# Item loads of an RWKV attention stage: one long row per partition split into two shorter pieces

## The chip, the core and the metric

The kernel runs on one core of a Trainium2 chip. The core has a matrix engine (TensorE, PE in the profile; its weight loads are listed as PEld), a vector engine (VectorE, DVE), a scalar engine (ScalarE, ACT), GpSimd (POOL) and SyncE (SP), which here does nothing but issue DMAs. Sixteen DMA engines move data between HBM (the chip's main memory) and SBUF (the on-chip memory, 128 partitions), and they also bring the engines' own instructions. PSUM holds what PE writes. The metric is the device time of one execution in microseconds, as the median of several runs.

## What is computed

Two blocks follow each other. The first is a linear attention with a decaying state (RWKV-5), for B = 4 sequences, H = 8 heads, S = 768 tokens and D = 48 channels per head:

```python
for t in range(S):
    kt, vt, rt = (k[:, :, t], v[:, :, t], r[:, :, t])
    cur = np.einsum('bhd,bhe->bhde', u[None] * kt, vt)
    y[:, :, t] = np.einsum('bhd,bhde->bhe', rt, state + cur)
    state = w[None, :, :, None] * state + np.einsum('bhd,bhe->bhde', kt, vt)
```

Its output, with heads side by side, is x with 384 channels per token. The second block is a mixture of experts with a gate that keeps neighbours together:

```python
fresh_e = int(np.argmax(logits[b, s]))
if s == 0 or local_gate[b, s] < 0.5:
    e = fresh_e
else:
    e = prev_e if prev_e >= 0 else fresh_e
...
h = np.maximum(x[b, s] @ w1[e], 0.0)
out[b, s] = p[e] * (h @ w2[e])
```

There are 8 experts with 1024 hidden channels; p is the softmax of the token's 8 logits.

## The kernel before

**Two stages.** The first stage computes the attention, item by item, and routes the tokens of the first two sequences on the way. The second stage gathers tokens by expert and runs the experts' two matrix products; it is PE's alone, nearly without a gap. The order of the instructions on every engine is written out by hand (`tc.manual_schedule()`), so nothing is moved by a scheduler; an engine starts its next instruction when the semaphores that it waits for are there.

**Items.** An item is one sequence and one pair of heads: 4 x 4 = 16 items. The two heads of a pair lie in partitions 0 to 47 and 64 to 111 (padded to 64 each). The 768 tokens are cut into six chunks of 128. For each item the kernel needs three inputs, which the host lays out before the run:

- `rk`: r and k with channels in the partitions, 768 tokens of r and then 768 of k in a row: 6144 bytes per partition, 768 KB in all
- `kv`: k and v with tokens in the partitions, 576 numbers each and 16 of padding: 4672 bytes per partition, 584 KB
- `vT`: v with channels in the partitions, 3072 bytes per partition, 384 KB

**Loads.** `load(n)` (lines 194 to 206) issues the three DMAs of item n on SP's queue: rk (line 199, or for item 0 two halves, line 202), kv (line 203), vT (line 204). Items 0 to 2 are loaded at the start, and item n + 3 at the top of step n. There are four buffers each for rk and vT and five for kv. A load into a used buffer waits for the old item's last reader. Apart from that, SP's DMAs share eight completion semaphores in turn, so a load also waits for the landing of the DMA that was issued eight before it. Each load is cut by partitions over the 16 DMA engines, eight partitions each; in the packet records every partition's row is one packet, and each engine ends a DMA with a packet of 4 bytes for the semaphore.

**An item's work.** In the order of the data:

- POOL, `scale` (lines 208 to 229): `ke`, k times a decay (line 217, from kv, two halves); `rw`, r times a decay (line 234, from rk, two halves; for items 0 to 2 on DVE); `pd`, r times k (line 221, from rk, two halves). For items from 3 on the order is ke, rw, pd, one item ahead of PE.
- DVE, `keys`: `kw`, k times the inverse decay (line 241, from rk).
- PE, `added` (line 253, from ke and kv): each chunk's addition to the state; DVE, `states` (line 259): the scan over the chunks.
- PE, `scores` (line 289, from kw and rw): scores inside a chunk, in two halves of three chunks; DVE masks each half (line 291).
- PE, `own` (line 269, from pd) and DVE (line 274, with vT): the token's own term. It stands between the two halves of the scores from item 3 on.
- PE, `inside` (line 298, from the masked scores and kv) and `before` (line 311, from the state and rw); ACT and DVE copy the result out (line 315), PE transposes it (line 324), ACT copies it to x (line 326) and, once per sequence, stores x to HBM (line 329, on ACT's own DMA queue).

The instructions of one item run interleaved with those of its neighbours: step n has `added`, `keys` and `states` of item n, `scale` of item n + 1, `inside` and `before` of item n - 1, then `scores` and `own` of item n.

**Code.** PE alone has over 7,700 matmuls and weight loads. They are not repeated by a loop, so PE's program comes from HBM while it runs, as packets of 16 KB on a queue of their own (q8 in the profile).

**The rare path.** `general_attention` (from line 473) is run only when a decay lies outside the bounds of the fast path. It reads the same arrays and is not entered with this data.

Of the kernel before, what the change touches and what calls it, by code (L numbers as in the profile page):

```python
# [50 lines left out]
C2 = NCH // 2  # L51
AHEAD = 4
VB = NCH * 2 * DH


def spread(ap, axis, n):
# [5 lines left out]
class Attention:  # L62
# [13 lines left out]
    def __init__(self, tc, st, rk_d, kv_d, vT_d, x_d, w_t, wp_d, kept, ident, lt, mp):  # L76
        self.tc, self.nc = tc, tc.nc
        nc = tc.nc
        self.rk_d, self.kv_d, self.vT_d, self.x_d = rk_d, kv_d, vT_d, x_d
        self.w_t, self.kept, self.ident, self.lt = w_t, kept, ident, lt  # L80

        self.late = st.enter_context(tc.tile_pool(name="late", bufs=1))
        self.wp = self.late.tile([P, H, 32], F32, name="wp")
        self.sel = self.late.tile([P, 2 * (E + 1)], F32, name="sel")
        self.inner = ExitStack()

        def pool(name, bufs, **kw):
            return self.inner.enter_context(tc.tile_pool(name=name, bufs=bufs, **kw))

        once = pool("once", 1)  # L90
        self.two = pool("two", 2)
        self.three = pool("three", 3)
        ps = pool("ps", 1, space=PSUM)

        self.pairs = [ps.tile([P, 2, 512], F32, name=f"pair{i}") for i in range(2)]
        self.py = pool("py", 1, space=PSUM)

        self.T = mp[:, 2 * P + 2:2 * P + 2 + (NCH - 1) * DH].rearrange("p (e c) -> p e c", c=NCH - 1)

        self.inv = pool("pinv", 1, space=PSUM).tile([P, HP, P], F32, name="inv")  # L100


        n = B * HP - 1
        self.rks, self.vTs = [None] * AHEAD, [None] * AHEAD
        for i in range(1, AHEAD + 1):
            self.rks[(n + i) % AHEAD] = once.tile([P, 2, NCH, P], F32, name=f"rk{i}")
        for i in range(1, AHEAD + 1):
            self.vTs[(n + i) % AHEAD] = once.tile([P, 2, C2, P], F32, name=f"vT{i}")
        self.kvs = [once.tile([P, 2 * VB + DP - DH], F32, name=f"kv{i}") for i in range(AHEAD + 1)]
        self.items = [dict() for _ in range(B * HP)]  # L110
        self.xTs, self.xs, self.lTs = {}, {}, {}
        for i in range(AHEAD - 1):
            self.load(i)
        nc.sync.dma_start(out=self.wp, in_=wp_d)


        self.step = once.tile([P, HP, DH, NCH - 1], F32, name="step")
        nc.vector.memset(self.step, 0.0)


        self.tab = tab = once.tile([P, HP, 2, P + 1], F32, name="tab")
        nc.vector.memset(tab[:, 0, :, 0:1], 1.0)
        nc.gpsimd.memset(tab[:, 1:, :, 0:1], 1.0)
        w = once.tile([P, HP, 2], F32, name="w")
        nc.vector.tensor_scalar(w[:, :, 0], w_t[:, :, 0], W_LO, W_HI, Alu.max, Alu.min)
        nc.vector.reciprocal(w[:, :, 1], w[:, :, 0])
        nc.vector.tensor_copy(tab[:, 0, :, 1], w[:, 0])
        nc.gpsimd.tensor_copy(tab[:, 1:, :, 1], w[:, 1:])
        n = 2
        while n <= P:  # L130
            m = min(n - 1, P + 1 - n)
            for engine, t in ((nc.vector, tab[:, :1]), (nc.gpsimd, tab[:, 1:])):
                engine.tensor_mul(t[..., n:n + m], t[..., 1:1 + m], t[..., n - 1:n].to_broadcast([P, t.shape[1], 2, m]))
            n += m

        self.first, self.newton = mp[:, :P + 1], mp[:, P + 1:2 * P + 1]
        nc.scalar.copy(self.first, tab[:, 0, 0])
        self.reciprocals(0)

        self.end = once.tile([P, HP, P + DP], F32, name="end")  # L140
        self.endT = once.tile([P, 2, HP, 2 * DH], F32, name="endT")
        self.align(26)
        self.warm(8)
        self.ends(slice(0, 1))
        self.turn_ends(slice(0, 1))
        self.warm(5)
# [47 lines left out]
    def load(self, n):  # L194
        nc = self.nc
        b, hp = divmod(n, HP)
        rk, vT, kv = self.rks[n % AHEAD], self.vTs[n % AHEAD], self.kvs[n % (AHEAD + 1)]
        if n:
            nc.sync.dma_start(out=rk.rearrange("p a c t -> p (a c t)"), in_=self.rk_d[b, hp])
        else:  # L200
            for z in (slice(0, C2), slice(C2, NCH)):
                nc.sync.dma_start(out=rk[:, :, z], in_=self.rk_d[b, hp].rearrange("p (a c t) -> p a c t", a=2, c=NCH)[:, :, z])
        nc.sync.dma_start(out=kv, in_=self.kv_d[b, hp])
        nc.sync.dma_start(out=vT.rearrange("p a c t -> p (a c t)"), in_=self.vT_d[b, hp])
        self.items[n].update(b=b, hp=hp, rT=rk[:, 0], kT=rk[:, 1], vT=vT,
                             k=kv[:, :VB].rearrange("p (c x) -> p c x", c=NCH), v=kv[:, VB:])

    def scale(self, n):

# [263 lines left out]
def general_attention(tc, rk_d, kv_d, wu, wg_d, x_d, ident, lt):  # L473

    nc = tc.nc
    with tc.tile_pool(name="g1", bufs=1) as g1, tc.tile_pool(name="g2", bufs=2) as g2, \
# [9 lines left out]
        with tc.For_i(0, HP, 1) as hp:  # L486
            wu_t = g1.tile([P, 2], F32, name="g_wu")
            nc.sync.dma_start(out=wu_t, in_=wu[bass.ds(hp, 1)].rearrange("o p x -> (o p) x"))
            with tc.For_i(0, B, 1) as b:
                def of(ap):  # L490
                    return ap[bass.ds(b, 1), bass.ds(hp, 1)].rearrange("o q p x -> (o q p) x")

                r_t = g1.tile([P, S], F32, name="g_r")
                k_t = g1.tile([P, S], F32, name="g_k")
                v_t = g1.tile([P, NCH, 2, DH], F32, name="g_v")
                nc.sync.dma_start(out=r_t, in_=of(rk_d)[:, :S])
                nc.sync.dma_start(out=k_t, in_=of(rk_d)[:, S:])
                nc.sync.dma_start(out=v_t.rearrange("p c i e -> p (c i e)"),
                                  in_=of(kv_d)[:, 2 * NCH * DH:4 * NCH * DH])
                yp = gy.tile([P, 2, 512], F32, name="g_y")  # L500
                for e in range(DH):
                    vp = gps.tile([P, 2, 512], F32, name="g_vp")
                    for c in range(NCH):
                        for i in range(2):
                            nc.tensor.matmul(
                                vp[i * DP:(i + 1) * DP, c // 3, (c % 3) * P:(c % 3 + 1) * P],
                                lhsT=v_t[:, c, i, e:e + 1].to_broadcast([P, DP]),
                                rhs=turned if c % 2 else ident,
                                start=True, stop=True)
                    kv = g2.tile([P, S], F32, name="g_kv")  # L510
                    nc.vector.tensor_mul(kv.rearrange("p (g t) -> p g t", g=2),
                                         k_t.rearrange("p (g t) -> p g t", g=2), vp[:, :, :3 * P])
                    sv = g2.tile([P, S + 1], F32, name="g_sv")
                    nc.vector.memset(sv[:, 0:1], 0.0)
                    nc.vector.tensor_tensor_scan(sv[:, 1:], wu_t[:, 0:1].to_broadcast([P, S]), kv, 0.0,
                                                 Alu.mult, Alu.add)
                    z = g2.tile([P, S], F32, name="g_z")
                    nc.vector.scalar_tensor_tensor(z, kv, wu_t[:, 1:2], sv[:, :S], Alu.mult, Alu.add)
                    nc.vector.tensor_mul(z, z, r_t)
                    for c in range(NCH):  # L520
                        o = (c % 3) * 2 * DH + 2 * e
                        nc.tensor.matmul(yp[:, c // 3, o:o + 2], lhsT=z[:, c * P:(c + 1) * P], rhs=ones,
                                         start=True, stop=True)
                y = g1.tile([P, 2, 3, 2, DH], F32, name="g_ys")
                for g in range(2):
                    for i in range(2):
                        nc.vector.tensor_copy(
                            y[:, g, :, i, :],
                            yp[:, g, :6 * DH].rearrange("p (c e i) -> p c e i", c=3, i=2)[:, :, :, i])
                nc.sync.dma_start(  # L530
                    out=x_d.rearrange("(b c p) (h j) -> b h p c j", b=B, p=P, h=HP)
                    [bass.ds(b, 1), bass.ds(hp, 1)].rearrange("o q p c j -> (o q p) c j"),
                    in_=y.rearrange("p g c i e -> p (g c) (i e)"))
# [1113 lines left out]
def _rows(a, np):  # L1647

    x = np.pad(a.transpose(0, 1, 3, 2), ((0, 0), (0, 0), (0, DP - DH), (0, 0)))
    return x.reshape(B, HP, P, S)  # L1650
# [50 lines left out]
```

## Time and profile before

| what | value |
|---|---|
| median of 3 runs | 389.7 us (389.01 to 390.44) |
| the profiled execution | 389.11 us |
| its span, first instruction to last | 387.0 us |
| busy: PE, PEld | 369.1 us (95%), 329.6 us (85%) |
| busy: DVE, ACT, POOL | 256.5, 102.9, 150.7 us |
| DMA in the whole span | 17477 packets, 74.97 MB |
| SP's queue (q1) | 10048 packets, 56.89 MB |
| ACT's queue (q10), GpSimd's (q0) | 7.87 MB, 9.52 MB |
| instruction queue q8 | 32 packets, 0.52 MB |
| rk, kv, vT: issue to landing, median | 9.8, 8.9, 8.1 us |
| last item load issued, landed | 85.14, 90.11 us |

How to read it: the span is what the trace covers, from the first of the program's instructions to the last; the execution's own time is 2.1 us longer. A line such as L217 is line 217 of the kernel. In a timeline a row has a start, a duration, the engine, the line, the operation and what it writes and reads; in square brackets stands how long the engine was idle before it, and who ended the wait ("issue" is idle time for which the profile finds no releaser). The granted clock is the share of PE's full clock that the chip allowed. A DMA's packets are listed by queue; the trace also keeps for every packet its queue, size, start and duration.

### The profile page before, as it was taken

The numbers are of one execution on the slowest core, as the hardware profiler recorded it, in microseconds if no ns is written. First come the engines' busy times: TensorE is split into PE (matmuls) and PEld (weight loads), VectorE is DVE, ScalarE is ACT, GpSimd is POOL, SyncE is SP. The second block draws the span as 40 slices with busy tenths as digits, with TensorE's granted clock in tenths as the row PEclk, the third lists the DMA queues.
The fourth block names the chain that finished last, engine by engine and source line by source line (L and its number), as shares of the span: only waits on it lengthen the run. The fifth ranks groups of instructions, "written<-read, shape, count | busy, mean of one in ns | idle before, by whom it ended". The sixth has DMA issues, their size and how long they took to land. (4 is left out here: it accounts for less than half of the span.)

```text
span 387.0 us, 9749 instructions
## 1 busy us (share of the span) xinstructions
PE 369.1 (95%) x3858; PEld 329.6 (85%) x3858; DVE 256.5 (66%) x749; ACT 102.9 (27%) x293; POOL 150.7 (39%) x212
## 2 busy tenths in 40 slices
PE   8998999799989999999999999999999999999992
PEld 7776876677868999998999999999999999999971
DVE  6997686899974573587647757757767758556400
ACT  4121221122213111322323243234224234222220
POOL 8769999696322022611233212312403213112022
PEclk9999999999999999999999999999999999999997
DMA  7999998989212982640453145245156146064011
GB/s 266 413 409 411 405 403 272 315 294 400 86 31 94 374 337 75 246 189 23 184 167 120 41 169 205 74 171 203 55 185 224 38 163 225 23 200 182 2 37 36
DMA packets 17477, 74.97 MB, mean 194 GB/s; under 512 B 2729, under 2 KB 6586, under 8 KB 14864
## 3 DMA queue, kind: packets, MB, share of 16 engines
q1 hardware_dynamic: 10048, 56.89, 39.4%
q0 software_dynamic: 3424, 9.52, 7.4%
q10 hardware_dynamic: 3952, 7.87, 5.6%
q8 instruction: 32, 0.52, 0.5%
q14 instruction: 21, 0.17, 0.1%
HBM read 64.83 MB, written 9.51 MB: 192 GB/s over the span
## 5 line engine op out<-in xcount | busy, mean ns | idle before, releaser
L1259 POOL DMA_INDIRECT out_dram<-yo,sid x27 | 26.7, 988 | 102.7 <-ACT yo L1254 79.0
L1110 PE MATMUL h<-exT,w1t 128*128 128x168 f32 (+4 forms) x240 | 54.9, 327 | 0.0
L1114 DVE TENSOR_TENSOR hT<-h,hs 128x168 f32<-128x168 f32 (+3 forms) x60 | 21.1, 351 | 46.4 <-PE h L1110 30.0
L1033 POOL DMA_INDIRECT xg<-x_d,gid x29 | 31.2, 1076 | 39.3 <-DVE sm L868 17.4
L1110 PEld LDWEIGHTS h<-exT,w1t 128*128 128x128 f32 x240 | 41.6, 190 | 0.3 <-issue 0.3
L1060 PE MATMUL h<-exT,w1t 128*128 128x192 f32 (+1 forms) x192 | 38.2, 337 | 0.0
L1179 PE MATMUL y<-factors,sums 128*128 128x192 f32 x168 | 36.8, 326 | 0.0
L1110 PE MATMUL h<-xs,ws 128*128 128x168 f32 (+4 forms) x144 | 35.3, 326 | 0.0
L1060 PEld LDWEIGHTS h<-exT,w1t 128*128 128x128 f32 x192 | 32.3, 190 | 1.4 <-issue 0.2
L221 POOL TENSOR_TENSOR pd<-rk 128x384 f32<-128x384 f32 x32 | 31.4, 1002 | 2.3 <-DMA rk<-in_rk_dram 2.3
L291 DVE TENSOR_TENSOR am<-pair,kept 128x768 f32<-128x768 f32 x32 | 30.3, 949 | 1.4 <-PE pair L289 1.4
L1110 PEld LDWEIGHTS h<-xs,ws 128*128 128x128 f32 x144 | 25.5, 190 | 4.3 <-ACT hs L1117 1.2
L1179 PEld LDWEIGHTS y<-factors,sums 128*128 128x128 f32 x168 | 28.9, 190 | 0.0
L289 PEld LDWEIGHTS pair<-rw,kw 48*64 48x64 f32 x768 | 23.7, 133 | 5.4 <-issue 1.6
L289 PE MATMUL pair<-rw,kw 48*64 48x64 f32 (+1 forms) x768 | 26.4, 249 | 1.2 <-issue 1.0
L234 POOL TENSOR_TENSOR rw<-rk,tab 128x384 f32<-128x384 f32 x26 | 23.6, 926 | 8.2 <-PE y L311 8.2
L217 POOL TENSOR_TENSOR ke<-kv,endT 128x288 f32<-128x288 f32 x32 | 24.9, 797 | 4.3 <-DMA kv<-in_kv_dram 3.0
L298 PE MATMUL y<-am,kv 128*64 128x128 f32 x384 | 25.3, 276 | 0.5 <-DVE am L291 0.4
L1179 PE MATMUL y<-w2t,hT 128*128 128x192 f32 x96 | 23.0, 328 | 0.0
L298 PEld LDWEIGHTS y<-am,kv 128*64 128x64 f32 x384 | 21.0, 137 | 1.9 <-DVE am L291 0.9
L1047 DVE COPY exT<-tp 128x384 f32<-128x384 f32 (+6 forms) x29 | 14.0, 488 | 12.8 <-PE tp L1046 12.6
L1165 DVE TENSOR_TENSOR factors<-w2t 128x192 f32<-128x192 f32 x56 | 19.7, 351 | 0.0
(279 smaller groups left out, 733.5 us busy)
## 6 DMA issues: line engine op xcount, KB each, us to landing
w1t<-in_w_dram SPq DMA_DIRECT2D x9, 1536.0 KB, 6.7
w2t<-in_w_dram SPq DMA_DIRECT2D x9, 1536.0 KB, 6.9
rk<-in_rk_dram SPq DMA_DIRECT2D x15, 768.0 KB, 9.8
kv<-in_kv_dram SPq DMA_DIRECT2D x16, 584.0 KB, 8.9
vT<-in_vT_dram SPq DMA_DIRECT2D x16, 384.0 KB, 8.1
x_d<-x ACTq DMA_DIRECT2D x4, 1152.0 KB, 8.6
w1t<-in_w_dram ACTq DMA_DIRECT2D x1, 1536.0 KB, 10.5
w2t<-in_w_dram ACTq DMA_DIRECT2D x1, 1536.0 KB, 13.6
```

The lines of the kernel that those rows point to most:

```text
L217: nc.gpsimd.tensor_mul(t["ke"][:, p::2], t["k"][:, p::2], spread(self.endT[:, p, hp], 1, C2))
L221: nc.gpsimd.tensor_mul(t["pd"][:, z], t["rT"][:, z], t["kT"][:, z])
L234: engine.tensor_mul(t["rw"][:, z], t["rT"][:, z], spread(pw, 1, z.stop - z.start))
L289: nc.tensor.matmul(sc[f * DP:(f + 1) * DP, h, i, x:], lhsT=t["kw"][q, c, o * DP:(o + 1) * DP], rhs=t["rw"][q, c, x:], start=True, stop=True)
L291: return lambda: nc.vector.tensor_mul(t["am"][:, g], sc, spread(self.kept[:, g:g + 3], 1, 2))
L298: nc.tensor.matmul(t["y"][h][p * DP:(p + 1) * DP, c2 * P:(c2 + 1) * P], lhsT=t["v"][:, (2 * c + h) * DH:(2 * c + h) * DH + DP], rhs=t["am" ...
L1033: self.nc.gpsimd.indirect_dma_start(out=xg[:n], out_offset=None, in_=self.x_d[:rows], in_offset=bass.IndirectOffsetOnAxis(ap=u["gid"][:n, ...
L1060: nc.tensor.matmul(h[:, :n], lhsT=u["w1"][:, m, kk, :], rhs=u["xT"][:, kk, :], start=(kk == 0), stop=(kk == DK - 1))
L1110: nc.tensor.matmul(out, lhsT=a, rhs=b, start=start and k == 0, stop=stop and k == len(terms) - 1, skip_group_check=True)
L1114: nc.vector.tensor_tensor(out, a, b, op=Alu.add)
L1179: return lambda: nc.tensor.matmul(bank[:, x * half:(x + 1) * half], lhsT=a, rhs=b, start=(j == 0 and x == 0), stop=(j == FK // 2 - 1), ski ...
L1259: self.nc.gpsimd.indirect_dma_start(out=out.rearrange("n (h d) -> (n h) d", h=2) if half else out, out_offset=bass.IndirectOffsetOnAxis(ap ...
```

## The change

The arrays `rk` and `kv` get an axis of two ahead of the partition axis in HBM: all of r's rows, then all of k's; all of k's token rows, then all of v's. In SBUF nothing moves in rk, and each of kv's two parts gets its own 16 numbers of padding, so that a kv row has 4736 bytes in place of 4672. A load is still one DMA, but a partition's row now comes from two places, as two pieces: 2 x 3072 bytes for rk, 2 x 2368 for kv. Item 0's rk, which was already cut into pieces of 1536 bytes, keeps their size. vT is not touched, and no instruction of PE, DVE, ACT or POOL and no wait is added, removed or moved.

```diff
 VB = NCH * 2 * DH
+VW = VB + DP - DH
...
-        self.kvs = [once.tile([P, 2 * VB + DP - DH], F32, name=f"kv{i}") for i in range(AHEAD + 1)]
+        self.kvs = [once.tile([P, 2, VW], F32, name=f"kv{i}") for i in range(AHEAD + 1)]
...
         if n:
-            nc.sync.dma_start(out=rk.rearrange("p a c t -> p (a c t)"), in_=self.rk_d[b, hp])
+            nc.sync.dma_start(out=rk.rearrange("p a c t -> p a (c t)"), in_=self.rk_d[b, hp].rearrange("a p x -> p a x"))
         else:
             for z in (slice(0, C2), slice(C2, NCH)):
-                nc.sync.dma_start(out=rk[:, :, z], in_=self.rk_d[b, hp].rearrange("p (a c t) -> p a c t", a=2, c=NCH)[:, :, z])
-        nc.sync.dma_start(out=kv, in_=self.kv_d[b, hp])
+                nc.sync.dma_start(out=rk[:, :, z], in_=self.rk_d[b, hp].rearrange("a p (c t) -> p a c t", c=NCH)[:, :, z])
+        nc.sync.dma_start(out=kv, in_=self.kv_d[b, hp].rearrange("a p x -> p a x"))
         nc.sync.dma_start(out=vT.rearrange("p a c t -> p (a c t)"), in_=self.vT_d[b, hp])
         self.items[n].update(b=b, hp=hp, rT=rk[:, 0], kT=rk[:, 1], vT=vT,
-                             k=kv[:, :VB].rearrange("p (c x) -> p c x", c=NCH), v=kv[:, VB:])
+                             k=kv[:, 0, :VB].rearrange("p (c x) -> p c x", c=NCH), v=kv[:, 1])
...
-        "rk": _np.concatenate([_rows(i["r"], _np), _rows(i["k"], _np)], 3),
-        "kv": _np.pad(_np.concatenate([_tokens(i["k"], _np), _tokens(i["v"], _np)], 3),
-                      ((0, 0), (0, 0), (0, 0), (0, DP - DH))),
+        "rk": _np.stack([_rows(i["r"], _np), _rows(i["k"], _np)], 2),
+        "kv": _np.pad(_np.stack([_tokens(i["k"], _np), _tokens(i["v"], _np)], 2), ((0, 0),) * 4 + ((0, DP - DH),)),
```

The reads of the rare path are adapted to the new arrays in the same way.

More of the change, by code (lines that the diff above doesn't have):

```diff
@@ L489, in general_attention, with of @@
             with tc.For_i(0, B, 1) as b:
-                def of(ap):
-                    return ap[bass.ds(b, 1), bass.ds(hp, 1)].rearrange("o q p x -> (o q p) x")
+                def of(ap, a):
+                    return ap[bass.ds(b, 1), bass.ds(hp, 1)].rearrange("o q a p x -> a (o q p) x")[a]
                 r_t = g1.tile([P, S], F32, name="g_r")
@@ L495, in general_attention @@
                 v_t = g1.tile([P, NCH, 2, DH], F32, name="g_v")
-                nc.sync.dma_start(out=r_t, in_=of(rk_d)[:, :S])
-                nc.sync.dma_start(out=k_t, in_=of(rk_d)[:, S:])
+                nc.sync.dma_start(out=r_t, in_=of(rk_d, 0))
+                nc.sync.dma_start(out=k_t, in_=of(rk_d, 1))
                 nc.sync.dma_start(out=v_t.rearrange("p c i e -> p (c i e)"),
-                                  in_=of(kv_d)[:, 2 * NCH * DH:4 * NCH * DH])
+                                  in_=of(kv_d, 1)[:, :VB])
                 yp = gy.tile([P, 2, 512], F32, name="g_y")
```

## The prediction

> **What bounds the kernel now.** I read the page's busy rows and the 40 slices first, then a table of stretches of ten microseconds, then who waits for a DMA, then the timelines of POOL and PE. The chain of waits is no help: it holds 0.99 us from 380.31 on and goes no further back, so I follow the path by hand.
>
> The stretches (us; busy time of each engine, granted clock, DMA share, GB/s):
>
> ```profile
> 20.00:30.00 10.00, 9.42 (x217) 7.57 (x211) 9.48 (x20) 2.54 (x7) 7.56 (x9) 1.00 1.02 410
> 30.00:40.00 10.00, 8.82 (x175) 6.77 (x174) 7.35 (x11) 2.36 (x6) 10.00 (x18) 1.00 1.02 411
> ...
> 120.00:130.00 10.00, 10.00 (x66) 9.65 (x66) 4.04 (x21) 3.04 (x11) 2.40 (x4) 1.00 0.69 241
> ```
>
> From 120 us PE is busy without a gap, and item loads are over (the last is issued at 85.14). The change can act only on the stage of the sixteen items, up to about 117 us, where PE and DVE hand work to each other; a microsecond lost there is a microsecond at the end. The granted clock is 1.00 in every stretch, so it plays no part. Until about 58 us the DMA engines are full: 410 GB/s at a share of 1.02. Who waits for them?
>
> ```profile
> POOL ke L217 <- DMA kv<-in_kv_dram: 3.0, 2, 2.6
> ...
> POOL pd L221 <- DMA rk<-in_rk_dram: 2.3, 2, 1.2
> ```
>
> Among the item loads' readers only POOL, four times, before items 1 to 4. DVE and PE never wait for an item load. So a full DMA does not by itself set the end; it sets how much room POOL has.
>
> **Part 1: longer packets become twice as many.** An rk load had 8 packets of 6144 B on each of 16 DMA engines and gets 16 of 3072; a kv load had 8 of 4672 and gets 16 of 2368, 64 B a row more in all. Item 0's rk keeps its 1536 B packets. vT, the weights, the stores and every instruction of PE, DVE, ACT and POOL keep their order and their waits; SP issues the same DMAs in the same places. The price of a packet is in the trace's packet records. From 10 to 40 us the means are 239 ns for 6144 B, 182 for 4672 and 125 for 3072 (vT has that size already); 1536 B stores took 66 ns where they ran alone. So rk costs 8 x (2 x 125 - 239) = 0.08 us more on each engine. 2368 B lies on the line from 66 to 125 ns at 98 ns, so kv costs 8 x (2 x 98 - 182) = 0.11 us more. An item goes from about 4.33 us (1736 KB at 410 GB/s) to 4.5, 4% more. The bounds: nothing at all, since from landing to landing vT6, in 3072 B packets, took 0.96 us for 384 KB (410 GB/s), and the next rk, in 6144 B packets, 1.91 us for 768 KB (412); at the other end the 23 ns of the next paragraph. I take the 10 to 13 ns of the records.
>
> Where that lands:
>
> ```profile
> 22.07 1.55 POOL L217 TENSOR_TENSOR ke<-kv,endT 128x288 f32<-128x288 f32 x2 [2.65 <-DMA kv<-in_kv_dram]
> 23.58 1.69 POOL L234 TENSOR_TENSOR rw<-rk,tab 128x384 f32<-128x384 f32 x2
> 25.22 1.96 POOL L221 TENSOR_TENSOR pd<-rk 128x384 f32<-128x384 f32 x2
> 27.56 1.55 POOL L217 TENSOR_TENSOR ke<-kv,endT 128x288 f32<-128x288 f32 x2 [0.37 <-DMA kv<-in_kv_dram]
> ```
>
> Item 3's ke, rw and pd start when kv3 lands (21.91) and end at 23.62, 25.27 and 27.18. PE takes them at 24.99 (L253), 27.44 (L289) and 28.45 (L269): room 1.37, 2.17 and 1.27 us. By kv3 the stream carries three changed rk and four kv: 3 x 0.08 + 4 x 0.11 = 0.7 us late, inside 1.27. Item 4's ke ends at 29.11 and is taken at 30.71: room 1.60 against 0.85 us. After that POOL is never again idle for a DMA and runs ahead: pd of item 7 ends at 49.43, own terms of item 7 start at 54.47. So part 1 costs **nothing**, hidden by POOL's lead over PE. The cover goes at 1.27 us late, that is 1.27 us over 7 x 8 added packets = 23 ns each; beyond it each microsecond counts. SP's queue adds nothing: its loads wait for the landing of the DMA eight before, with the engines full behind it, and issues of 256 pieces took 0.59 to 0.67 us (item 0's rk), against 0.33 to 0.9 for 128.
>
> **Part 2: what else uses these DMA engines.** PE has two idle stretches that nothing releases ("issue"):
>
> ```profile
> 33.26 0.37 PE L289 MATMUL pair<-rw,kw 48*64 48x128 f32 x4
> 34.60 0.60 PE L289 MATMUL pair<-rw,kw 48*64 48x64 f32 x17 [0.97 <-issue]
> ...
> 58.49 0.47 PE L311 MATMUL y<-rw,S 48*48 48x128 f32 x6
> 59.72 0.58 PE L311 MATMUL y<-rw,S 48*48 48x128 f32 x11 [0.76 <-issue]
> ```
>
> Counted from the start, the first instruction after these gaps is PE's number 1218 and 2242, 1024 apart, and 16 KB instruction packets moved at 32.03 to 33.12 and 57.44 to 58.42:
>
> ```profile
> q1 hardware_dynamic: 125, 0.46, 96.9%
> q8 instruction: 1, 0.02, 5.7%
> ```
>
> (queues from 32.0 to 33.2 us). PE waited for its own code: 1.72 us in sum, and DVE waited behind it (1.14 us before L291 at 35.30), so this is on the path. If blocks of 256 instructions are asked for one block ahead, at every 256th instruction counted to these two, the nine fetches of the full stage waited 2.79, 3.21, 3.43, 4.27, 3.60, 2.70, 3.55, 4.32 and 3.32 us from asking to moving; with idle DMA engines (105.66 us) it was 0.34. After moving, a block needs about 1.0 us for the packet and 1.4 until PE goes on (1.48 and 1.30 at the two stalls). The stretches without their stalls last 6.6, 6.9, 5.95, 5.87, 7.1, 5.57, 5.84, 5.84 and 6.7 us, so they bear waits of 4.2, 4.5, 3.5, 3.5, 4.7, 3.2, 3.4, 3.4 and 4.3. Two went over, and three more were close.
>
> The wait is the queue of item packets on that engine. If it is a matter of bytes or whole DMAs, the change leaves it, plus the 4%. Each of the nine waits put into each of the stretches gives 1.25 us of stalls on average, and 1.8 with 0.15 us added, against 1.72 seen: -0.5 to +0.1 us, of which I take **-0.3**. If it is a number of packets, about 3 us is 16 of them at 180 ns (4.33 us over 24 per item); at 113 ns (4.5 over 40) the waits fall to at most 2.9 us and both stalls go: -1.7.
>
> [...]
>
> **The sum.** 0 for part 1, -0.3 for part 2. The profiled execution took 389.11 us (span 387.0 and 2.1 around it), so 388.8 for one like it; the three runs have a median of 389.7, 0.6 above it, and on that scale the forecast is **389.4**.
>
> **Rivals.** Times on the median's scale; a measurement of this kernel tells about 0.3% (1.2 us) from no change.
> - *Fetch waits count packets, and shrink.* For: a store, issued at 39.66 into the full queue, moved its first packet at 43.2, as late as the code, so another queue does wait behind something already lined up. Against: a block asked for at 93.75, under weight loads of 12288 B (0.46 us each), moved after 1.9 us, where 16 packets would be 7.4. Price: both stalls, -1.7: 388.0, and 387.6 at the low end of the runs' own scatter (389.01 to 390.44 about 389.7).
> - *Fetch waits get longer.* The place is the same: the twice as many pieces ahead of a code block cost more than their bytes. At 0.45 us more per wait (13%) the same average gives 3.1 us of stalls, 1.4 more than seen: 391.1. That is where it passes 0.3%. For: five stretches have hardly room. Against: only 4% more time per item in the records.
> - *The stream comes too late for POOL.* Above 23 ns per added packet PE waits at items 3 and 4; at 44 ns it is 2.5 us late, 1.2 past the room: 390.9, and 391.7 at 58 ns. For: POOL already waits there. Against: 10 to 13 ns from the records.
> - *It does nothing visible.* vT's pace equals rk's, and the stalls fall as they did: 389.7, in the first case's range.
>
> **How the numbers follow.** Forecast with the last rival, within 0.3%: 0.38 (388.6 to 390.5). Shrinking waits, faster: 0.32. Longer waits, slower: 0.18; late stream, slower: 0.12. Faster 0.32, same 0.38, slower 0.30. Both signs hold much, so the range takes in both: 387.6 from the second case's low end to 392.0 just above the late stream's 391.7.
>
> **What would show it.** Part 1 is right if kv3 lands at 22.2 to 22.8 and POOL's ke starts there, with PE's L253 of item 3 still near 25.0 and no DVE or PE wait on a load. The packet prices are right if 3072 B keep 121 to 125 ns and 2368 B take 95 to 100. Part 2 shows in PE's unreleased gaps of 0.5 us and more before 70 us: in sum 1.2 to 1.8 for the forecast, none for shrinking waits, over 3 for longer ones; and in the moment at which each 16 KB packet moves after PE passes its block. The prediction is wrong if DVE waits for rk or vT in the first 20 us, if engines idle while SP has loads to issue, or if the stage from 117 us on changes its length.

## The result and the profile after

| | median | runs |
|---|---|---|
| before | 390.81 us | 6 (389.01 to 393.47) |
| after | 396.73 us | 6 (394.13 to 398.13) |
| forecast | 389.4 us | 387.6 to 392.0 |

After stands to before as 1.0139, with a 95% interval of 1.0099 to 1.018: slower by 5.9 us, where 389.4 us, no change that can be seen, was forecast. (The ratios in this document are formed over the single runs, without those more than 1.5% above the fastest of their kernel; so they can differ from the quotient of the two medians beside them.) The profiled execution of after took 397.32 us, 8.2 more than that of before.

**The end moved as a whole.** In the table of stretches, the 270 us that begin 1.0 us before DVE's last copy to `xT` (line 315 before, at 116.96 us; line 316 after, at 125.24) have the same PE work to the last digit in both kernels: 263.59 us in 1694 matmuls. After:

```profile
124.29:394.29 270.00, 263.59 (x1694) 244.88 (x1693) 161.32 (x555) 76.24 (x217) 63.81 (x89) 0.99 0.41 145
```

Before, with a start of 116.00:

```profile
116.00:386.00 270.00, 263.59 (x1694) 244.88 (x1693) 161.35 (x555) 76.36 (x217) 63.92 (x89) 0.99 0.41 145
```

So all 8.2 us were lost in the stage of the items. To find out where, I lined up one event per item: the start of DVE's own terms (line 275 after, 274 before).

| item | before, us | after, us | later by |
|---|---|---|---|
| 0 | 10.30 | 13.58 | 3.28 |
| 1 | 16.43 | 21.10 | 4.67 |
| 2 to 6 | 23.30 to 49.72 | 27.98 to 54.41 | 4.68 to 4.69 |
| 8 | 62.02 | 67.51 | 5.49 |
| 9 | 70.02 | 76.77 | 6.75 |
| 10 | 77.90 | 86.15 | 8.25 |
| 15 | 113.04 | 121.33 | 8.29 |

More than half is lost before item 1 is done, most of it on item 0, whose rk pieces kept their size; from item 1 to item 6, where the stream of item loads is fullest, nothing is added. Now the head of the timeline, SP, ACT and DVE, before:

```profile
0.82 1.31 SPq L202 DMA_DIRECT2D rk<-in_rk_dram  x2
0.82 0.43 ACTq L1577 DMA_DIRECT2D w_t<-in_wu_dram  x1
...
2.81 0.17 DVE L125 TENSOR_SCALAR w<-w_t 128x4 f32<-128x4 f32 x1 [0.85 <-DMA w_t<-in_wu_dram]
```

and after:

```profile
0.82 0.96 SPq L203 DMA_DIRECT2D rk<-in_rk_dram  x2
0.82 0.49 ACTq L1578 DMA_DIRECT2D w_t<-in_wu_dram  x1
...
4.77 0.17 DVE L126 TENSOR_SCALAR w<-w_t 128x4 f32<-128x4 f32 x1 [2.81 <-DMA w_t<-in_wu_dram]
```

`w_t` holds the decays, 4 KB in 512 pieces of 8 bytes; ACT issues it at the very start, and everything DVE, ACT and PE do with the decay tables follows from it. Line 1578 was not touched. Yet its data is used 1.96 us later. What came between shows in the DMA queues' table from 1.8 to 2.8 us (packets, MB, share of 16 engines; q1 is SP's queue, q10 ACT's). Before:

```profile
q10 hardware_dynamic: 528, 0.00, 28.2%
q1 hardware_dynamic: 29, 0.04, 27.0%
```

After:

```profile
q1 hardware_dynamic: 64, 0.10, 61.7%
```

Before, all 528 packets of `w_t` (512 pieces and 16 for the semaphore) moved in this microsecond, ahead of nearly all of rk. After, not one did; they moved between 2.8 and 4.3 us, mixed with 334 packets of SP's queue, rk's. The first issue of rk decides it. It took 0.668 us before and ended at 1.49, after ACT's (1.25). After the change it took 0.446 us and ended at 1.262, ahead of ACT's 1.308. Each of these two rk loads still has 256 pieces of 1536 bytes: only the addresses in HBM changed.

What the late tables then do to PE:

```profile
4.46 1.49 PE L165 MATMUL pair<-ident 128*128 128x128 f32 x8
7.84 0.47 PE L175 MATMUL pair<-ident,end 128*128 128x128 f32 x2 [1.90 <-ACT end L168]
```

and before:

```profile
4.46 1.97 PE L164 MATMUL pair<-ident 128*128 128x128 f32 x8
6.22 0.63 PE L174 MATMUL pair<-ident,end 128*128 128x128 f32 x2
```

PE idles for 1.90 us between its warm-up transposes and the first work on the tables, where it had no gap before. In the stretches (columns as in the prediction: busy PE, PEld, DVE, ACT, POOL, then the granted clock), after:

```profile
0.00:10.00 10.00, 5.99 (x79) 5.47 (x83) 5.38 (x18) 3.88 (x11) 6.37 (x24) 0.94 0.81 282
10.00:20.00 10.00, 9.78 (x167) 7.60 (x163) 6.60 (x14) 1.96 (x6) 8.27 (x10) 0.72 1.04 400
20.00:30.00 10.00, 9.09 (x193) 6.36 (x187) 9.21 (x18) 2.06 (x6) 7.36 (x10) 1.00 1.04 402
```

and before, the second of them:

```profile
10.00:20.00 10.00, 9.42 (x191) 7.19 (x191) 9.11 (x19) 1.39 (x3) 7.07 (x9) 1.00 1.02 412
```

The clock, 1.00 here in the kernel before, falls to 0.72 in the second row: the clock records show half speed from 8.73 to 15.55 us. PE looks busier (9.78 against before's 9.42) and does less (167 matmuls against 191): busy time at a low clock is not work. Later the page's row of clocks shows two more dips, at 66.75 to 70.17 and 80.41 to 83.82 us:

```profile
PEclk9799998989999999999999999999999999999997
```

Two PE gaps come shortly before them:

```profile
64.93 0.58 PE L312 MATMUL y<-rw,S 48*48 48x128 f32 x11 [1.04 <-issue]
...
80.51 0.38 PE L676 MATMUL mp<-ident,key 128*12 128x128 f32 x1 [1.94 <-DVE key L669]
```

The second was there before the change too (1.90 us at 71.82), with the clock at full speed.

**The stream of item loads**, which the prediction was about, did almost what it said: kv3 landed at 22.01 us (21.91 before; 22.2 to 22.8 forecast), and POOL took it there:

```profile
22.16 1.56 POOL L218 TENSOR_TENSOR ke<-kv,endT 128x288 f32<-128x288 f32 x2 [1.34 <-DMA kv<-in_kv_dram]
```

The stream started earlier, since rk went ahead of `w_t`, and then ran slower: kv0's last packet moved at 7.13 us in place of 7.80, and from there to kv3's last it took 14.29 us in place of 13.43. With PE 4.7 us late, kv3 was early enough by far.

### The profile page after: what moved, and what is told of

The parts are those of the page before. It is cut to its first block, busy times and chain, and to the rows that moved or that the text cites. A ratio compares the mean times of both kernels' runs of the same rounds, so it can differ in the third digit from the quotient of the medians.

```text
span 395.3 us, 9749 instructions
## 1 busy us (share of the span) xinstructions
PE 374.4 (95%) x3858; PEld 332.9 (84%) x3858; DVE 256.9 (65%) x749; ACT 102.8 (26%) x293; POOL 151.3 (38%) x212
## 5 line engine op out<-in xcount | busy, mean ns | idle before, releaser
L290 PEld LDWEIGHTS pair<-rw,kw 48*64 48x64 f32 x768 | 25.4, 141 | 6.0 <-issue 1.7
L290 PE MATMUL pair<-rw,kw 48*64 48x128 f32 (+1 forms) x768 | 28.1, 262 | 1.8 <-issue 1.0
L299 PE MATMUL y<-am,kv 128*64 128x128 f32 x384 | 26.6, 285 | 0.6 <-DVE am L292 0.4
L299 PEld LDWEIGHTS y<-am,kv 128*64 128x64 f32 x384 | 22.2, 142 | 2.0 <-DVE am L292 0.9
```

The costliest lines, as they stand in the source:

```text
L290: nc.tensor.matmul(sc[f * DP:(f + 1) * DP, h, i, x:], lhsT=t["kw"][q, c, o * DP:(o + 1) * DP], rhs=t["rw"][q, c, x:], start=True, stop=True)
L299: nc.tensor.matmul(t["y"][h][p * DP:(p + 1) * DP, c2 * P:(c2 + 1) * P], lhsT=t["v"][:, (2 * c + h) * DH:(2 * c + h) * DH + DP], rhs=t["am" ...
```

## The experiments

Two theories. **The start:** the new place of item 0's rk in HBM shortens SP's first issue, rk's packets get ahead of `w_t`'s, the tables come 2 us late, and PE's idle time then costs it its clock. The rival, **the stream:** twice as many pieces make the item loads and the code blocks late, and the head is a chance of one profile. The kernel before scatters too, so each comparison has its own runs of it on the same chip.

### One half of the change each

e1 splits only rk (kv's array, tile and load as before):

```diff
-        self.kvs = [once.tile([P, 2, VW], F32, name=f"kv{i}") for i in range(AHEAD + 1)]
+        self.kvs = [once.tile([P, 2 * VB + DP - DH], F32, name=f"kv{i}") for i in range(AHEAD + 1)]
...
-        nc.sync.dma_start(out=kv, in_=self.kv_d[b, hp].rearrange("a p x -> p a x"))
+        nc.sync.dma_start(out=kv, in_=self.kv_d[b, hp])
```

> rk split in two pieces, kv whole as before. Theory A (the loss begins with the decay table's load w_t, which lands at 4.75 us after and 2.79 before because rk's first pieces go ahead of it; PE then idles 1.9 us at about 6 us and its clock is halved until 15.6): if it is rk's new place in HBM that lets item 0's rk go ahead, w_t lands near 4.7 here too, own terms of item 0 (DVE line 274) start near 13.5 in place of 10.3, and the time is 4 to 7 us above before. Theory B (the doubled kv pieces behind rk crowd out w_t): w_t lands near 2.8 and the time is within 1.5 us of before. Theory C (who goes first is chance): w_t lands early or late by luck, and the runs scatter between 389 and 398.

Measured: 395.45 us (4 runs) beside 391.81, ratio 1.0104 [1.0049, 1.0159]. SP's first issue took 0.446 us, `w_t` was used at 4.64 us, the own terms of item 0 started at 12.87.

e2 splits only kv:

```diff
-            nc.sync.dma_start(out=rk.rearrange("p a c t -> p a (c t)"), in_=self.rk_d[b, hp].rearrange("a p x -> p a x"))
+            nc.sync.dma_start(out=rk.rearrange("p a c t -> p (a c t)"), in_=self.rk_d[b, hp])
...
-                nc.sync.dma_start(out=rk[:, :, z], in_=self.rk_d[b, hp].rearrange("a p (c t) -> p a c t", c=NCH)[:, :, z])
+                nc.sync.dma_start(out=rk[:, :, z], in_=self.rk_d[b, hp].rearrange("p (a c t) -> p a c t", a=2, c=NCH)[:, :, z])
```

> kv split in two pieces, rk whole as before. Theory A with rk as the cause: w_t lands near 2.8, own terms of item 0 start near 10.3, time within 1.5 us of before. Theory B (kv's pieces): w_t near 4.7 and 4 to 7 us above before. Theory C: by luck.

Measured: 392.42 us (10 runs) beside 391.81, ratio 1.0018 [0.9981, 1.0056]; first issue 0.673 us, `w_t` used at 2.79, own terms of item 0 at 10.28. kv adds as many pieces to the stream as rk does, so the loss isn't a matter of their number: it goes with rk, and with the start.

### Only item 0's rk

e6 is the kernel before, with item 0's two rk loads, and nothing else, from an extra copy in the new layout. e5 is the reverse: the kernel after, with these two loads from a copy in the old layout. The edit of e6:

```diff
-                nc.sync.dma_start(out=rk[:, :, z], in_=self.rk_d[b, hp].rearrange("p (a c t) -> p a c t", a=2, c=NCH)[:, :, z])
+                nc.sync.dma_start(out=rk[:, :, z], in_=self.rk0.rearrange("a p (c t) -> p a c t", c=NCH)[:, :, z])
...
+        "rk0": _np.stack([_rows(i["r"], _np), _rows(i["k"], _np)], 2)[0, 0],
```

> The kernel before, all rows whole, with item 0's two rk loads alone taken from a copy in the new layout. Theory A: these two DMAs are enough: SP's first issue 0.45 us, w_t lands near 4.7, own terms of item 0 start at 12.8 to 13.6, and the time is 394 to 397. Rival (it takes the later pieces too): w_t near 2.8, 390 to 393.

Measured: 395.04 us (10 runs) beside 391.08 (31 runs), ratio 1.0073 [1.0029, 1.0116]. Its timeline and stretch:

```profile
0.81 0.96 SPq L202 DMA_DIRECT2D rk<-in_rk_dram  x2
0.82 0.49 ACTq L1578 DMA_DIRECT2D w_t<-in_wu_dram  x1
...
4.69 0.17 DVE L125 TENSOR_SCALAR w<-w_t 128x4 f32<-128x4 f32 x1 [2.73 <-DMA w_t<-in_wu_dram]
```

```profile
10.00:20.00 10.00, 9.77 (x164) 7.60 (x161) 6.46 (x14) 1.89 (x6) 8.18 (x11) 0.71 1.02 409
```

The short issue, the late `w_t`, the low clock and the late own terms (13.49 and 21.16 us for items 0 and 1) are all there, with whole rows in all of the later stream. This is the most direct test of the start theory. In the time it is 4.0 us by the medians and 2.9 us by the ratio, with an interval of 1.1 to 4.5 us.

> The changed kernel, with item 0's two rk loads alone taken from a copy in the old layout (their pieces are 1536 bytes in both); all other rk loads and all kv loads stay in two pieces. Theory A (the issue of item 0's rk, shorter in the new layout, passes w_t's): SP's first issue is back at 0.67 us, w_t lands near 2.8, own terms of item 0 start near 10.3, and the time is 391 to 394, as with w_t first on SP (393.2). Rival (the split of later loads crowds out w_t): w_t near 4.7, 395 or more.

Measured: 392.78 us (10 runs) beside 391.08, ratio 1.0052 [1.0019, 1.0086].

```profile
0.82 1.32 SPq L203 DMA_DIRECT2D rk<-in_rk_dram  x2
...
3.24 0.17 DVE L126 TENSOR_SCALAR w<-w_t 128x4 f32<-128x4 f32 x1 [1.28 <-DMA w_t<-in_wu_dram]
```

With the old addresses the issue is long again and `w_t` is ahead, but for a tail of 11 packets after 2.8 us. Own terms of item 0 start at 10.68. Of the 5.9 us, 1.7 by the medians and 2.0 by the ratio remain, so that some 4 are gone.

### w_t out of the race

If the order of two queues is the cause, `w_t` as the first load on SP's own queue removes it. e4 and e10 are this on the kernel after, e9 on the kernel before:

```diff
-    nc.scalar.dma_start(out=w_t, in_=wu.rearrange("h p x -> p h x"))
+    nc.sync.dma_start(out=w_t, in_=wu.rearrange("h p x -> p h x"))
```

> The changed kernel with w_t's load as the first DMA of SP's queue, ahead of item 0's rk, in place of ACT's queue. Theory A: w_t lands by 3.0 us, PE has no gap of over 0.6 us before 16 us, the clock stays full, and the time is within 1.5 us of the kernel before (389 to 392): the whole loss gone, though every rk and kv load is still in two pieces. Rival (pieces cost in the stream): still 3 us or more above before.

Measured: 393.22 us (10 runs) beside 391.81, ratio 1.0049 [1.0016, 1.0082]; `w_t` used at 2.82, own terms at 10.27 and 16.43 us, which are the times of before. But the own terms of item 3 start at 30.05, 0.65 late, and the time lies above the 389 to 392 us that the start theory alone had asked for.

> The kernel before, whole rows, with w_t's load first on SP's queue, so that no two queues start together. Beside the next run it shows the price of the pieces alone. Theory A (after w_t is put right, pieces cost by the later stream and by code waits): 390 to 392, about as before. Rival (w_t on SP, with rk behind it, costs by itself): 392.5 or more, like the changed kernel with w_t on SP (393.2).

> The changed kernel with w_t first on SP, again, on the same chip as the run before this one. Theory A: 1 to 2.5 us above that run; item 3's ke starts 1 to 2 us later than with whole rows, PE's unreleased gaps before 70 us are 2.2 to 2.6 us in sum against 1.6 to 1.9. Rival (pieces cost nothing): within 0.7 us of that run.

Measured on one chip, 12 runs each: e9 391.94 us, ratio to before 0.9995 [0.997, 1.0021]; e10 393.13, ratio 1.0034 [1.0002, 1.0067]. The means of e10 and e9 lie 1.6 us apart (resampled, 0.6 to 2.7). With the head put right in both, this is what is left of the change, pieces and new addresses together. Some 0.5 us of it may be the clock: its mean is 0.9891 over e10's runs and 0.9906 over e9's, and on this chip the time of the kernel before goes by 3.45 us for 0.01 (35 runs). Where is the rest? POOL and PE around item 3, e9:

```profile
22.69 1.57 POOL L217 TENSOR_TENSOR ke<-kv,endT 128x288 f32<-128x288 f32 x2 [2.67 <-DMA kv<-in_kv_dram]
...
24.99 0.66 PE L253 MATMUL mp<-kv,ke 128*48 128x48 f32 x20 [0.46 <-issue]
```

and e10:

```profile
24.09 1.56 POOL L218 TENSOR_TENSOR ke<-kv,endT 128x288 f32<-128x288 f32 x2 [3.02 <-PE mp L254]
...
25.16 0.29 PE L254 MATMUL mp<-kv,ke 128*48 128x48 f32 x4 [0.46 <-POOL ke L218]
25.70 0.56 PE L254 MATMUL mp<-kv,ke 128*48 128x48 f32 x16 [0.25 <-POOL ke L218]
...
29.28 0.88 PE L270 MATMUL y<-pd,w_t 48*64 48x384 f32 x8 [0.40 <-POOL pd L222]
```

`ke` of item 3 starts 1.4 us later (the releaser PE named in the first row had long been done; it is the load of kv), and PE now waits for POOL in all three rows, where e9 has only a gap of 0.46 us without a releaser. Half of the 1.4 is there when kv0's last packet moves (8.19 against 7.46 us), the other half is lost from kv0 to kv3 (15.27 us against 14.60). At the own terms 0.84 us of it is left for item 3 (30.25 against 29.41) and 0.67 for item 4. PE's gaps without a releaser, which the prediction read as waits for its code, come on top: 2.64 us in sum in e10, 1.88 in e9, in which the last of these rows is the main one (e10, then e9):

```profile
55.57 0.58 PE L312 MATMUL y<-rw,S 48*48 48x128 f32 x12 [1.32 <-issue]
```

```profile
59.99 0.58 PE L311 MATMUL y<-rw,S 48*48 48x128 f32 x11 [0.76 <-issue]
```

### w_t later in the kernel before

e3 puts a memset of `w_t` ahead of its load, so that the load waits for it:

```diff
-    nc.scalar.dma_start(out=w_t, in_=wu.rearrange("h p x -> p h x"))
...
+    nc.vector.memset(w_t, 0.0)
+    nc.scalar.dma_start(out=w_t, in_=wu.rearrange("h p x -> p h x"))
```

> The kernel before, whole rows, with w_t's load issued some 0.4 us later (behind a first write to the same tile), so that item 0's rk is issued ahead of it. Theory A (a late w_t is enough, packet sizes of the item loads do not matter): w_t lands 1 to 2.5 us later than 2.79, PE idles between its warming transposes and line 174, the clock falls to a half in the first 16 us, and the time is 4 to 8 us above before, as with the change. Rival (the pieces themselves cost in the stream): at most 2 us above before, the delay of w_t itself.

Measured: 392.43 us (10 runs) beside 391.81, ratio 1.0016 [0.9983, 1.0048]. ACT's issue moved only to 0.99 us and ended at 1.438, still ahead of SP's 1.488, so `w_t` was used at 3.58, 0.77 late; own terms of item 0 came 0.71 late, PE's gap was 1.05 us, and the clock stayed full at the head. The lateness meant to be made was not made, so the run says little about its price. It does agree on the order: the issue that ended first was served first, though with a lead of 0.05 us 52 of the 512 pieces moved after 2.8 us.

### w_t in fewer pieces

e7 (on before) and e8 (on after) load `w_t` as 128 rows of 32 bytes from an array laid out for it:

```diff
-    nc.scalar.dma_start(out=w_t, in_=wu.rearrange("h p x -> p h x"))
+    nc.scalar.dma_start(out=w_t.rearrange("p h x -> p (h x)"), in_=wt)
```

> The kernel before, with w_t laid out by the host as 128 rows of 32 bytes in place of 512 pieces of 8. Theory A (the path to the first item starts at w_t's landing): w_t's issue gets shorter, it lands up to 0.5 us before 2.79, and the time falls by as much, 0 to 1 us. Rival (who is first is decided by something else than the number of pieces): no change in the landing, within 0.5 us of before.

Measured: 390.49 us (10 runs) beside 391.08, ratio 0.9983 [0.9953, 1.0013]. ACT's issue took 0.380 us, `w_t` was used at 2.43, own terms of item 0 started at 9.66, 0.64 earlier than before.

> The changed kernel with w_t as 128 rows of 32 bytes. Theory A (the issue that ends first goes first; the margin was 46 ns): w_t's issue ends ahead of item 0's rk, it lands by 2.8, and the time is 391 to 394. [...]

Measured: 392.31 us (10 runs) beside 391.08, ratio 1.0045 [1.0016, 1.0075]. Here the two issues ended within 0.02 us of each other (1.245 and 1.261); `w_t` was used at 3.60, later than the 2.8 that was expected and earlier than the 4.77 of after, own terms of item 0 at 11.03.

> The kernel before with w_t as 128 rows of 32 bytes, again, in more runs: w_t landed at 2.41 in place of 2.79, and item 0's own terms started 0.64 us earlier. Theory A: 0.3 to 0.8 us below before, the interval at or just clear of no change. Rival: no difference.

Measured, e7's kernel once more: 391.9 us (12 runs) beside 391.99 (35 runs), ratio 0.9989 [0.996, 1.0018]. Its trace repeats only part of the gain: `w_t` was used at 2.59 us and own terms of item 0 started at 10.08, 0.22 earlier than before in place of 0.64. In the time neither run tells the gain from nothing.

### The clock by itself

e11 is the kernel after with more warm-up transposes, which fill PE's gap at the head; `w_t` stays late. (The 14 transposes are 28 more instructions of PE, so the blocks of its code begin at other places behind them.)

```diff
-        self.warm(8)
+        self.warm(22)
```

> The changed kernel with 22 warming transposes in place of 8 ahead of line 174, so that PE does not idle while it waits for the late w_t. w_t still lands near 4.75. Theory A (part of the loss is PE's clock at a half after the idle 1.9 us): the clock stays full until 30 us, own terms of item 1 start near 19 in place of 21.1, and the time is 1.5 to 3.5 us below the changed kernel: 393 to 395. Rival (the clock is no part of it): within 1 us of 396.7.

Measured: 393.77 us (12 runs) beside 391.99, ratio 1.0029 [0.9999, 1.0059].

```profile
4.46 3.24 PE L165 MATMUL pair<-ident 128*128 128x128 f32 x22
7.65 0.47 PE L175 MATMUL pair<-ident,end 128*128 128x128 f32 x2
```

```profile
10.00:20.00 10.00, 9.57 (x197) 6.86 (x191) 8.92 (x18) 1.77 (x5) 8.89 (x11) 1.00 1.04 401
```

PE has no gap, the clock stays at 1.00, and 197 matmuls pass in the second stretch in place of 167, though `w_t` was used at 4.57. Own terms of item 1 start at 18.18, 1.75 us later than before where the kernel after was 4.67 late. So a table that is used 1.76 us late (4.57 against 2.81) makes item 1 1.75 us late. In after it was used 1.96 us late; so some 1.95 of the 4.67 us are the late table, and the other 2.7 the clock. I had expected about 19; the clock took more of it than I gave it. By the ratios to the kernel before, on two chips, 1.1% of the 1.4% is gone (4.3 us), which is more than the 2.7 us; e11's mean clocks are 0.985 to 0.995 over its runs, after's 0.977 to 0.991.

The profile shows one thing more about the clock. Its records begin at 7.08 us in before, 5.32 in after and 10.97 in e1, and a stretch ahead of the first record counts as 1.00. PE was at half speed there: up to the first record the transposes start 0.21 us apart, from it on 0.11 (which is why the same eight take 1.97 us in before and 1.49 in after). In e1 this half speed reached into item 0, and its item 1 was 2.57 us late with a table used 1.83 us late. How much the head loses to the clock thus differs from one kernel's profile to the next.

## Why the prediction was wrong, point by point

**The step that failed** is in part 1: "DVE and PE never wait for an item load. So a full DMA does not by itself set the end", and with it "SP's queue adds nothing". With "Item 0's rk keeps its 1536 B packets" and "SP issues the same DMAs in the same places" the first microseconds were put at nothing. At 2.8 us DVE did wait for a DMA, 0.85 us for `w_t`; it is no item load, so the sentence was true and the conclusion wrong. That wait was on the path, ended by 512 tiny packets which shared the DMA engines with item 0's rk, whose lines were in the diff. I counted its pieces (unchanged) and quoted its issue at "0.59 to 0.67 us", but took that as fixed by the number of pieces. It went to 0.446, `w_t` was used 1.96 us later, and item 1 came 4.67 us late.

**The second** is "The granted clock is 1.00 in every stretch, so it plays no part." It described the kernel before, and there only what lies behind the first clock record at 7.08 us. The new wait took PE's work away for 1.90 us at 6 us, and half speed for 6.83 us followed: some 2.7 us, more than the wait itself.

**Packet prices: right, near enough.** By the packet records from 10 to 40 us, 3072 bytes took 128 ns on average and 2368 bytes 97 (medians 124 and 95), where the working had 125 and 98. 11.79 MB took SP's queue 102.3% of 10 to 40 us:

```profile
q1 hardware_dynamic: 4643, 11.79, 102.3%
```

Before:

```profile
q1 hardware_dynamic: 3091, 12.23, 101.1%
```

That is 5.0% more time per byte, 4% forecast.

**Late stream, hidden: right in after, for a reason that I didn't give.** The head's lateness was larger than any cover asked for. The cover of 1.27 us itself was sized well: in e4 and e10 `ke` of item 3 started 1.8 and 2.0 us later than in before, and the own terms 0.65 and 0.85 later, so 1.15 us was hidden. Too small was the lateness: 0.7 us forecast, and 0.7 measured from kv0 to kv3, but 0.7 more came from the start of the stream. So the rival "The stream comes too late for POOL" is what happens once the head is put right: item 3 is 0.65 to 0.85 us late there, where that rival had 1.2.

**Part 2: the mechanism right, the value not.** Over the nine code blocks of the full stage the wait from asking to moving, by the prediction's count of instructions (the profile shows the moving, not the asking), was 3.47 us on average before and 3.35 after. Over all kernels it is 3.52 in the six with whole rows (before, e3, e6, e7, e9, e12: 3.26 to 3.74) and 3.65 in the eight with pieces (3.25 to 3.94; e1 and e2 have them in half of the loads). The difference is about the 4% of bytes and packet prices, but the two ranges overlap, and the counting isn't exact (in e8 one block moved 0.3 us before the moment at which it should have been asked for). "Fetch waits count packets", which wanted them a third shorter, has fallen. The step that failed is the size: "of which I take -0.3". It leaned on the average of 1.25 us that shuffled waits gave, and held the 1.72 seen for bad luck. Kernels with whole rows have 1.58 to 2.41 us of stalls, 1.90 on average; those with pieces (e1 and e2 in one load of each item) 2.13 to 3.49, 2.57 on average, or 2.44 without e11, whose code blocks lie elsewhere. So it is +0.5 to +0.7, not -0.3; my own working gave +0.55 for 0.15 us longer waits (1.8 against 1.25), and I set it against a wrong level. One profile each and a wide spread: the sign is likely, the size is not settled.

**The sum, by what was measured.** The profiled execution is 8.2 us longer: 4.67 at the head, which e11 parts into some 1.95 for the late table and 2.7 for the clock, and some 3.5 from item 7 to item 10, where the two later dips and a gap of 1.04 us lie, which I take for a code stall (a 16 KB instruction packet moved at 62.42 to 63.41 us, and PE went on at 64.93). Across the first of these dips the own terms fall back by 1.26 us (item 8 to item 9), across the second by 1.50 (item 9 to item 10). In e2, e3, e5 and e10, which each have one such dip at about 75 to 80 us, they fall back by 1.25 to 1.61 us from item 9 to item 10. The dips are not in every execution: the mean granted clock of after's six runs goes from 0.977 to 0.991, and in the kernel before the time falls by 3.25 to 3.85 us for each 0.01 that the clock is higher (25, 31 and 35 runs on three chips). A dip of 3.41 us takes 0.0044 off that mean, so 1.4 to 1.7 us, which agrees. What brings them on isn't shown, so neither is how many of them the change has to answer for; that the median's 5.9 us are these losses with fewer dips is likely. e5 and e6 show that 3 to 4 of the 5.9 us hang on item 0's rk alone.

**What stays open.** Why the issue of the same 256 pieces takes 0.446 us with the new addresses and 0.668 with the old was not tried. The load's own pieces are not all of it: kv0's issue, the next but one, took 0.59 to 0.60 us in every kernel with item 0's rk at the old addresses and 0.46 to 0.48 in every one with the new, whether kv itself was whole or in pieces. Later rk loads, issued into a full queue, show no such gain (0.37 us after, 0.33 before). And the 1.1 to 2.0 us that remain with a good head (e4, e5, e10) are shared between the late stream, the code stalls and the clock only by one profile of each kernel.

## What to carry to other kernels

Before asking what a change does to the full stage, follow the first microseconds: which small load does the first compute wait for, and what else is issued beside it on another queue; here a race of two issues that ended 0.23 us apart was turned by one issue 0.22 us shorter and the other 0.06 longer. Putting the load that everything hangs on first on the same queue as its competitor took it out of the race (`w_t` used at 2.82 us in e4 and e9, 2.91 in e10, where after had 4.77); fewer packets helped in part (3.60 in e8), and so did keeping PE occupied over the wait (item 1 at 18.18 us in e11, 21.10 in after). A granted clock of 1.00 in the profile of before said nothing of a longer wait (0.72 from 10 to 20 us in after), and nothing of the time ahead of its first record, at 7.08 us.

## What the runs showed of the hardware

- **Whose issue ended first was served first.** `w_t` went ahead where ACT's issue ended 0.23 to 0.29 us before SP's (before, e2, e5, e7, e12), and mostly at 0.05 us (e3); at 0.02 us (e8) it came in between, used at 3.60; and where SP's issue ended first, by 0.05 us, it came 1.8 to 2.0 us late (after, e1, e6, e11). The first packets of the queue that went first moved 0.60 to 0.67 us after its issue ended. So the choice of queue set the order, with 2 us at stake; on SP's own queue `w_t` came first whatever rk's addresses (2.82 us in e4 and e9, 2.91 in e10).
- **The clock's grid.** The clock's changes in after (8.73, 15.55, 66.75, 70.17, 80.41, 83.82 us) lie on multiples of 3.41 us from each other. In the 3.41 us ahead of each of these three falls PE was idle for 1.90 (5.32 to 8.73), 1.17 (63.34 to 66.75) and 1.84 us (77.00 to 80.41). Gaps of 1.05 us (e3, at 5.60) and 1.90 (before, at 71.82) left the clock full, those of 1.90 (after, at 5.95), 1.68 (e6, at 6.08) and 1.03 (after, at 63.90) did not, so the length of one gap alone doesn't tell them apart. Whether it matters where in the grid a gap falls, which would also make the time scatter between executions of one kernel, is not shown: no run tests it.
